# Softmax weights transposed by DMA in a window-attention and SoLU-MoE kernel

## The chip, the cores and the metric

The kernel runs on one core of a Trainium2 chip. Its time is the device time of one execution in microseconds, and the time before is the median of three runs. The profile comes from one further execution of the same program. TensorE is called PE there, its weight load PEld, VectorE DVE, ScalarE ACT, GpSimd POOL and SyncE SP; SP issues all DMAs of this kernel.

## The reference

A sliding-window attention (8 batches, 8 heads, 576 positions, head size 64, window 64) feeds a feed-forward block without residual (4608 tokens, 512 to 1024 to 512), all in float32:

```python
scores = scale * np.matmul(q, k.transpose(0, 1, 3, 2))
mask = (rel >= 0) & (rel < window)          # rel = pos[:, None] - pos[None, :], window = 64
scores = np.where(mask, scores, -1000000000.0)
scores = scores - np.max(scores, axis=-1, keepdims=True)
attn = np.exp(scores)
attn = attn / (np.sum(attn, axis=-1, keepdims=True) + 1e-09)
x = np.matmul(attn, v)                      # heads side by side: 4608 x 512
...
h = x @ w_in
e = np.exp(h - np.max(h, axis=-1, keepdims=True))
solu = h * e / (np.sum(e, axis=-1, keepdims=True) + 1e-09)
ln = (solu - mean) / np.sqrt(var + 1e-06) * g_ln
out = ln @ w_out
```

## The kernel before

The 4608 tokens are worked through in 36 tiles of 128. A query block of 64 sees 128 keys, so a tile's scores for one head are 128 x 128: two halves of 64 queries, each with its own shift of the keys and the values.

For each tile t the stages are these. **load** brings q (256 KB), k (384 KB) and two shifts of v (v0, v1, 256 KB each) by four DMAs. **scores** multiplies on TensorE into PSUM (pS). **softmax** takes row maxima on DVE (into sS), exponentials on ACT with row sums (sm), the reciprocal on DVE (rec), and scales sS head by head on POOL (L401). **transposes** turns the eight 128 x 128 heads on TensorE (t, L417), and ACT and DVE copy four each to SBUF (PT, L422). **values** multiplies PT with v into pX; ACT and DVE split the result into a rounded part xH and a rest xL. **moe_in** is two times 12 matmuls of 512 columns (high and low parts of x and of w_in) into pH. **moe_norm** is exp, product, squares and the layer norm, on DVE, ACT and POOL, and leaves e. **planes** takes e, 128 x 1024 float32, apart into two planes of 16-bit halves (pl; one half of the columns on DVE, one on POOL, L538). **turn** writes the planes to DRAM (yd, L545) and reads them back with a transposing DMA of 16-bit elements (yT, L548). **moe_transpose** splits yT into yH (ACT) and yL (DVE), **moe_out** is 24 matmuls into pO, ACT copies them to ot, and a DMA writes y.

The weights are 64-bit words in DRAM; eight blocks (raw, 1 MB each) are loaded and rebuilt as float32 by ACT and DVE at the start, and split into high and low parts a little later.

What sets the order is a planner, class `Plan`. Every stage is recorded with an engine, a cost in nanoseconds, the tiles it reads and writes, and a latency. Due times follow from the order on TensorE, and each engine's free slot goes to the ready work that is due first. Two lists were kept in the order of recording, TensorE's and SP's: `last` in `edges` holds both. `RINGS` gives the number of buffers of each tile. In the steady loop, iteration t records load(t+4), turn(t-1), the first half of moe_in(t), transposes(t+1), the second half, moe_norm(t) and planes(t), moe_transpose(t-2), values(t+1), scores(t+3), softmax(t+3) and moe_out(t-2).

Of the kernel before, what the change touches and what calls it, by code (L numbers as in the profile page):

```python
# [11 lines left out]
BF16 = mybir.dt.bfloat16  # L12
# [6 lines left out]
P = 128  # L19
# [25 lines left out]
}  # L47

# [1 line left out]
class Plan:  # L50
# [17 lines left out]
    def edges(self):  # L68

        before = [dict() for _ in self.ops]  # L70
        writer, readers, users, last = {}, {}, {}, {"PE": None, "SP": None}
        for i, (engine, _, _, reads, writes, _, loose) in enumerate(self.ops):
            for key in reads + writes:
                if key in writer:
                    before[i][writer[key]] = True
            for key in writes:
                for j in readers.pop(key, ()):
                    before[i][j] = True
                writer[key] = i
# [24 lines left out]
        return before  # L104
# [56 lines left out]
def tile_window_attention_solu_moe(  # L161
    ctx: ExitStack,
    tc: tile.TileContext,
    NBLK: int,
    qT: bass.AP,
    kT: bass.AP,
    v: bass.AP,
    w_in: bass.AP,
    w_out: bass.AP,
# [9 lines left out]

    nc = tc.nc  # L180

    NPAIR, _, NT = qT.shape
    DM = out.shape[1]
    w_in, w_out = w_in.bitcast(I32), w_out.bitcast(I32)
    DFF = w_in.shape[1] // 2
# [123 lines left out]

    def Q(t):
        return T("q", t, [P, NPAIR, P])

    def K(t):
        return T("k", t, [P, NPAIR, P + WIN])

    def V(t, half):
        return T(f"v{half}", t, [P, DM])

    def load(t, parts=range(4)):
        first = first_of(t)
        o = t * P

        lack = 0 if t else WIN
        if 0 in parts:
            plan.dma(P * P * 16, lambda: nc.sync.dma_start(
                Q(t), qT[:, :, o:o + P].rearrange("p d s -> d p s")), [], [("q", t)])
        if 1 in parts:
            plan.dma(P * P * 24, lambda: nc.sync.dma_start(  # L330
                K(t)[:, :, lack:], kT[:, :, o - WIN + lack:o + P].rearrange("p d s -> d p s")),
                [], [("k", t)])


        for half in range(2):
            i = o + (half - 1) * WIN
            if 2 + half not in parts:
                continue
            if first == half:
                for x in range(2):  # L340
                    plan.dma(P * P * 8, lambda x=x, half=half, i=i: nc.sync.dma_start(
                        V(t, half)[x * WIN:(x + 1) * WIN], v[i + WIN:i + P]),
                        [], [(f"v{half}", t, x)])
            else:
                plan.dma(P * P * 16, lambda half=half, i=i: nc.sync.dma_start(
                    V(t, half), v[i:i + P]), [], [(f"v{half}", t, x) for x in range(2)])
# [7 lines left out]
    def scores(t):  # L354
# [18 lines left out]
        plan.op("PE", 1000, emit, [("q", t), ("k", t)], [("pS", t)], loose=t < LOOSE)  # L373

    def softmax(t):
        def cols(tag, h):
# [23 lines left out]
        for h in range(H):  # L400
            plan.op(engine, cost, lambda h=h: v.tensor_scalar(  # L401
                SS(t)[:, h], SS(t)[:, h], rec()[:, h:h + 1], 0.0, ALU.mult, ALU.add),
                [("rec", t)], [("sS", t, h)])
# [30 lines left out]
    def values(t):  # L434
        def emit():
            for p in range(NPAIR):
# [46 lines left out]
    def moe_norm(t):  # L483
# [5 lines left out]
        def key(x):  # L489
# [42 lines left out]
    def planes(t):  # L532
        if not crosses(t):
            return
        for h in range(2):
            hs = slice(h * 512, (h + 1) * 512)
            engine, eng, cost = (("DVE", nc.vector, 1100), ("POOL", nc.gpsimd, 1300))[h]
            plan.op(engine, cost, lambda h=h, hs=hs, eng=eng: eng.tensor_copy(  # L538
                PL(t)[:, :, hs], E(t)[:, hs].bitcast(U16).rearrange("p (n k) -> p k n", k=2)),
                [("e", t, h)], [("pl", t, h)])  # L540

    def turn(t):
        if not crosses(t):
            return
        plan.dma(P * DFF * 4, lambda: nc.sync.dma_start(  # L545
            YD(t).rearrange("(p k) n -> p (k n)", k=2), PL(t).rearrange("p k n -> p (k n)")),
            [("pl", t, h) for h in range(2)], [("yd", t)])
        plan.op("SP", 4000, lambda: nc.sync.dma_start_transpose(  # L548
            YT(t).rearrange("p a b -> p (a b)").bitcast(U16).rearrange("p (a b) -> p a b", a=NF), YD(t)),
            [("yd", t)], [("yT", t)], 3000)  # L550

    def YH(t):
        return T("yH", t, [P, NF, P], F32 if t < PLAIN_OUT else F32R)
# [87 lines left out]
    for t in range(NTILE + BEHIND):  # L641
# [9 lines left out]
        if t < BEHIND:  # L651
            on(moe_in, t, 1)
            on(moe_norm, t)
            on(planes, t)
            on(transposes, t + 1)
            on(scores, t + AHEAD)
            on(softmax, t + AHEAD)
            on(values, t + 1)
        else:
            on(transposes, t + 1)  # L660
            on(moe_in, t, 1)
            on(moe_norm, t)
            on(planes, t)
# [47 lines left out]
```

## Time and profile before

| | |
|---|---|
| median of three runs | 571.24 us (570.96 to 571.53) |
| the profiled execution | 570.42 us, span 568.6 us |
| granted TensorE clock, mean | 0.985 |
| busy: PE, DVE, ACT, POOL | 537.1, 366.9, 322.1, 260.5 us |
| DMA: share of 16 engines by queue q1 | 57.1% |

A row of the groups reads: line, engine, operation, tile written <- tiles read, shapes, count | busy time in us, mean ns of one | idle time before it, and what ended that. A row of the chain: start, time, what. SPq rows are DMA issues: start, time of the issue on SP. A row of the windows: the stretch, its length, busy time of PE, PEld, DVE, ACT and POOL with counts, the granted clock, the DMA share and GB/s. Waits read: who waited <- for whom: total, times, longest.

### The profile page before, as it was taken

The page shows a single profiled execution, that of the slowest core. Times are in us where ns is not written, and L with a number is a line of the kernel's source. Part 1 is how long each engine was busy: PE and PEld are TensorE (multiplying, and loading weights), DVE is VectorE, ACT ScalarE, POOL GpSimd, SP SyncE. Part 2 cuts the span into 40 slices and gives each one's busy share as a digit, 9 for nine tenths or more (in the row PEclk, how much of TensorE's full clock was granted, in tenths as well). Part 3 has the DMA queues.
Part 4 walks back from the last instruction along what each step waited for, and adds up shares of the span by engine and source line. Part 5 has one row for each costly group of instructions (what it writes and reads, how often), then busy time and mean ns, then how long its engine had stood idle before and what let it go on. Part 6 is the DMA issues. An engine that isn't in the chain of part 4 may idle for free.

```text
span 568.6 us, 12131 instructions
## 1 busy us (share of the span) xinstructions
PE 537.1 (94%) x4312; PEld 420.1 (74%) x4312; DVE 366.9 (65%) x1198; ACT 322.1 (57%) x935; POOL 260.5 (46%) x439
## 2 busy tenths in 40 slices
PE   1587799999999999999999999999999999999997
PEld 1344368888888888888888888888888888888875
DVE  2968896666666666666666666666666666665540
ACT  3549785556555555555555555555555555554431
POOL 2036266554555545444455455555545555555310
PEclk9969799999999999999999999999999999999999
DMA  8967256556665565556766655556666655643310
GB/s 254 353 235 209 79 175 167 177 144 187 170 173 177 150 200 152 173 166 186 204 145 191 178 169 172 172 165 174 169 177 177 178 177 176 177 130 92 93 39 37
DMA packets 128956, 95.56 MB, mean 168 GB/s; under 512 B 72448, under 2 KB 109312, under 8 KB 128384
## 3 DMA queue, kind: packets, MB, share of 16 engines
q1 hardware_dynamic: 128896, 94.79, 57.1%
q8 instruction: 34, 0.56, 0.5%
q14 instruction: 26, 0.21, 0.1%
HBM read 50.73 MB, written 26.74 MB: 136 GB/s over the span
## 4 chain that ended last, share of the span: by engine, by line
PE 90%; DVE 3%; DMA 2%; POOL 1%; ACT 1%; SPq 1%; issue 0%; POOLq 0%
PE pO L606 36%; PE pH L478 33%; PE pS L369 6%; PE pX L441 6%; PE t L417 5%; PE pH L467 3%; DMA raw<-w_in 2%; POOL sS L401 1%; PE pO L596 1%; DVE w L286 1%; DVE sS L382 1%; DVE w L280 0%; DVE w L284 0%; DVE e L498 0%; ACT w L279 0%
## 5 line engine op out<-in xcount | busy, mean ns | idle before, releaser
L401 POOL TENSOR_SCALAR sS<-sS,rec 128x128 f32<-128x128 f32 x280 | 146.9, 542 | 52.2 <-DVE rec L398 29.1
L511 POOL TENSOR_TENSOR mst<-mst,neghalf 128x1 f32<-128x1 f32 x36 | 20.2, 561 | 234.2 <-DVE mst L509 234.2
L387 ACT ACTIVATE sS<-sS,nmx 128x128 f32<-128x128 f32 x288 | 112.3, 391 | 15.2 <-DVE nmx L382 15.0
L606 PE MATMUL pO<-w_outH,yH 128*128 128x512 f32 x280 | 114.7, 410 | 0.6 <-ACT yH L584 0.6
L606 PE MATMUL pO<-w,yH 128*128 128x512 f32 x280 | 110.9, 396 | 0.0
L606 PE MATMUL pO<-w_outH,yL 128*128 128x512 f32 x280 | 110.2, 394 | 0.0
L478 PE MATMUL pH<-w_inH,xH 128*128 128x512 f32 x264 | 107.9, 409 | 0.0
L478 PE MATMUL pH<-w,xH 128*128 128x512 f32 x264 | 103.9, 397 | 0.0
L478 PE MATMUL pH<-w_inH,xL 128*128 128x512 f32 x264 | 103.8, 393 | 0.0
L538 DVE COPY pl<-e 128x1024 uint16<-128x1024 uint16 x33 | 49.1, 1487 | 60.6 <-POOL e L515 60.6
L422 ACT COPY PT<-t 128x512 f32<-128x512 f32 x39 | 22.7, 587 | 93.9 <-PE t L417 93.9
L451 ACT CAST xH<-pX 128x512 fp32r<-128x512 f32 x33 | 19.3, 586 | 84.8 <-PE pX L441 84.8
L606 PEld LDWEIGHTS pO<-w_outH,yH 128*128 128x128 f32 x280 | 52.5, 187 | 17.8 <-issue 5.2
L606 PEld LDWEIGHTS pO<-w_outH,yL 128*128 128x128 f32 x280 | 52.6, 188 | 13.8 <-DVE yL L586 0.9
L515 POOL TENSOR_SCALAR e<-e,mst 128x512 f32<-128x512 f32 x72 | 58.1, 815 | 6.7 <-DVE mst L512 6.3
L606 PEld LDWEIGHTS pO<-w,yH 128*128 128x128 f32 x280 | 52.7, 188 | 10.8
L478 PEld LDWEIGHTS pH<-w_inH,xL 128*128 128x128 f32 x264 | 49.6, 188 | 12.5 <-issue 0.2
L493 DVE TENSOR_REDUCE mst<-pH 128x1 f32<-128x1024 f32 x36 | 44.0, 1222 | 22.9 <-PE pH L478 22.6
L478 PEld LDWEIGHTS pH<-w_inH,xH 128*128 128x128 f32 x264 | 49.6, 188 | 11.4 <-issue 0.2
L478 PEld LDWEIGHTS pH<-w,xH 128*128 128x128 f32 x264 | 49.7, 188 | 10.1
L369 PE MATMUL pS<-k,q 64*64 64x128 f32 x1152 | 42.4, 288 | 15.3 <-DVE sS L401 10.5
L387 ACT ACTIVATION_READ_ACCUMULATOR sS<-sS,nmx 128x1 f32 x288 | 54.1, 188 | 0.0
(66 smaller groups left out, 781.8 us busy)
## 6 DMA issues: line engine op xcount, KB each, us to landing
yd<-pl SPq DMA_DIRECT2D x33, 512.0 KB, 4.1
v<-vS SPq DMA_DIRECT2D x64, 256.0 KB, 3.4
k<-kT SPq DMA_DIRECT2D x35, 384.0 KB, 4.7
q<-qT SPq DMA_DIRECT2D x36, 256.0 KB, 4.0
y<-ot SPq DMA_DIRECT2D x36, 256.0 KB, 2.9
raw<-w_in SPq DMA_DIRECT2D x4, 1024.0 KB, 8.8
raw<-w_out SPq DMA_DIRECT2D x4, 1024.0 KB, 6.9
v<-vS SPq DMA_DIRECT2D x16, 128.0 KB, 3.2
```

The lines of the kernel that those rows point to most:

```text
L369: nc.tensor.matmul(PS(t)[half * WIN:(half + 1) * WIN, r, p], q[rs, p, half * WIN:(half + 1) * WIN], keys, start=True, stop=True)
L387: plan.op("ACT", 390, lambda h=h: nc.scalar.activation(SS(t)[:, h], SS(t)[:, h], AF.Exp, bias=cols("nmx", h), scale=-1.0, accum_out=cols(" ...
L401: plan.op(engine, cost, lambda h=h: v.tensor_scalar(SS(t)[:, h], SS(t)[:, h], rec()[:, h:h + 1], 0.0, ALU.mult, ALU.add), [("rec", t)], [( ...
L417: nc.tensor.transpose(pA()[:, i], SS(t)[:, 4 * x + i], ident)
L422: (nc.vector.tensor_copy if x and t >= EARLY else nc.scalar.copy)(PT(t)[:, 4 * x:4 * x + 4], pA()),
L441: nc.tensor.matmul(PX(t)[r * D:(r + 1) * D, p, ks], V(t, half)[:, h * D:(h + 1) * D], PT(t)[:, h, ks], start=True, stop=True)
L478: plan.op("PE", 233, lambda n=n, c=c, x=x, w=w: nc.tensor.matmul(PH(t)[:, hs], x(t)[:, c], WH(c, h) if w is WH else WL(c)[:, h], start=(n ...
L493: plan.op("DVE", 1150, lambda: nc.vector.tensor_reduce(nmax(), PH(t), axis=AX.X, op=ALU.max, negate=True), [("pH", t)], [key(0)])
L511: plan.op("POOL", 560, lambda: nc.gpsimd.tensor_tensor(kk(), kk(), neghalf, op=ALU.pow), [], [key(5)])
L515: plan.op("POOL", 770, lambda h=h, hs=hs: nc.gpsimd.tensor_scalar(E(t)[:, hs], E(t)[:, hs], nmean(), kk(), ALU.add, ALU.mult), [key(4), ke ...
L538: plan.op(engine, cost, lambda h=h, hs=hs, eng=eng: eng.tensor_copy(PL(t)[:, :, hs], E(t)[:, hs].bitcast(U16).rearrange("p (n k) -> p k n" ...
L606: plan.op("PE", 233, lambda f=f, i=i, x=x, k=k, y=y, w=w: nc.tensor.matmul(PO(), y(t)[:, f], w(i, x), start=(f == k == 0), stop=(f == NF - ...
```

## The change

From tile 4 on the softmax weights take the way that e takes already: POOL copies sS into two 16-bit planes (pp), a DMA writes them to DRAM (pd), and a transposing DMA reads them back as PT. The TensorE transposes and the copies out of PSUM are left out for these tiles. Both halves of the e planes go to DVE. q and k come as one array, laid out per tile on the host, in one DMA (qk, 640 KB); so do the two shifts of v (v, 512 KB). SP loses its fixed order in the planner. Some rings and planner costs change, and the squares of moe_norm go into the pl buffer instead of one of their own.

```diff
 BY_DMA = (1, 2)
+SOFT_BY_DMA = 4
 RINGS = {
-    "raw": 3, "w": 9, "q": 3, "k": 3, "v0": 3, "v1": 3, "sS": 3, "PT": 2, ...
-    "e": 3, "pl": 2, "yd": 3, "yT": 2, "sq": 1, ...
+    "raw": 3, "w": 9, "qk": 3, "v": 3, "sS": 2, "pp": 2, "pd": 3, "PT": 2, ...
+    "e": 2, "pl": 2, "yd": 3, "yT": 2, ...
...
-        writer, readers, users, last = {}, {}, {}, {"PE": None, "SP": None}
+        writer, readers, users, last = {}, {}, {}, {"PE": None}
...
+        if 0 in parts:
+            plan.dma(P * P * 40, lambda: nc.sync.dma_start(QK(t), qk[t]), [], [("qk", t)])
+        if 1 in parts:
+            plan.dma(P * P * 32, lambda: nc.sync.dma_start(T("v", t, [P, 2, DM]), v[t]), [], [("v", t)])
...
+    def soft_planes(t):
+        if t < SOFT_BY_DMA:
+            return
+        for x in range(2):
+            engine, copy, cost = ("POOL", nc.gpsimd.tensor_copy, 1050)
+            plan.op(engine, cost, lambda x=x, copy=copy: copy(
+                PP(t)[:, :, 4 * x:4 * x + 4].rearrange("p k h n -> p k (h n)"),
+                SS(t)[:, 4 * x:4 * x + 4].rearrange("p h n -> p (h n)").bitcast(U16).rearrange("p (n k) -> p k n", k=2)),
+                [("sS", t, 4 * x + i) for i in range(4)], [("pp", t, x)])
+
+    def soft_turn(t):
+        if t < SOFT_BY_DMA:
+            return
+        plan.dma(P * H * P * 4, lambda: nc.sync.dma_start(
+            PD(t).rearrange("(p k) n -> p (k n)", k=2), PP(t).rearrange("p k h n -> p (k h n)")),
+            [("pp", t, x) for x in range(2)], [("pd", t)])
+        plan.op("SP", 2600, lambda: nc.sync.dma_start_transpose(
+            PT(t).rearrange("p a b -> p (a b)").bitcast(U16).rearrange("p (a b) -> p a b", a=H), PD(t)),
+            [("pd", t)], [("PT", t, x) for x in range(2)], 2000)
...
     def transposes(t):
+        if t >= SOFT_BY_DMA:
+            return
...
-            T("sq", t, [P, DFF], BF16), E(t), AF.Square, bias=nmean(), scale=1.0, accum_out=ss()),
-            H2 + [key(4)], [key(3), ("sq", t)], lat=300)
+            PL(t)[:, 0].bitcast(BF16), E(t), AF.Square, bias=nmean(), scale=1.0, accum_out=ss()),
+            H2 + [key(4)], [key(3), ("pl", t, 0), ("pl", t, 1)], lat=300)
...
-            engine, eng, cost = (("DVE", nc.vector, 1100), ("POOL", nc.gpsimd, 1300))[h]
+            engine, eng, cost = ("DVE", nc.vector, 700)
...
-        plan.op("SP", 4000, lambda: nc.sync.dma_start_transpose(
+        plan.op("SP", 2600, lambda: nc.sync.dma_start_transpose(
...
-            [("yd", t)], [("yT", t)], 3000)
+            [("yd", t)], [("yT", t)], 2000)
...
             on(transposes, t + 1)
+            on(soft_turn, t + AHEAD - 1)
             on(moe_in, t, 1)
...
             on(softmax, t + AHEAD)
+            on(soft_planes, t + AHEAD)
```

The diff shows little of where the instructions land. Three places show it. The first is SP's queue in a steady iteration, of before; names carry the tile's number and then a buffer's:

```order
L345 DMA v0_16_2432<-vS 128x512
L345 DMA v1_16_2438<-vS 128x512
L545 DMA yd_11_2447<-pl_11_2363 128x2048
L548 DMA_TRANSPOSE yT_11_2465<-yd_11_2447 128x8x256
L614 DMA y<-ot_10_2499 128x512
L327 DMA q_17_2515<-qT 128x4x128
L330 DMA k_17_2522<-kT 128x4x192
```

And of the change:

```order
L327 DMA v_17_2471<-vS 128x1024
L405 DMA pd_15_2488<-pp_15_2457 128x2048
L325 DMA qk_19_2507<-qk 128x1280
L408 DMA_TRANSPOSE PT_15_2524<-pd_15_2488 128x8x256
L623 DMA y<-ot_11_2529 128x512
L554 DMA yd_13_2561<-pl_13_2509 128x2048
L557 DMA_TRANSPOSE yT_13_2593<-yd_13_2561 128x8x256
```

There are seven DMAs as before, but two transposing ones, each behind the write that feeds it; y moved ahead of yd, and one load stands between pd and PT.

The second place is DVE between the statistics of a tile and the row maximum of the next, of before:

```order
L507 SCALAR_TENSOR_TENSOR mst_12_2410<-mst_12_2410 128x1
L509 TENSOR_SCALAR mst_12_2410<-mst_12_2410 128x1
L395 TENSOR_SCALAR rec_15_2504<-sm_15_2454 128x8
L398 RECIPROCAL rec_15_2504<-rec_15_2504 128x8
L512 TENSOR_TENSOR mst_12_2410<-mst_12_2410 128x1
L538 COPY pl_12_2534<-e_12_2434 128x2x512
L422 COPY PT_14_2536<-t_57_2529 128x512
L574 TENSOR_TENSOR yL_11_2552<-yT_11_2465,yH_11_2541 128x512 x2
L493 TENSOR_REDUCE mst_13_2581<-pH_13_2495 128x1
```

And of the change:

```order
L516 SCALAR_TENSOR_TENSOR mst_13_2431<-mst_13_2431 128x1
L518 TENSOR_SCALAR mst_13_2431<-mst_13_2431 128x1
L583 TENSOR_TENSOR yL_12_2532<-yT_12_2433,yH_12_2519 128x512
L521 TENSOR_TENSOR mst_13_2431<-mst_13_2431 128x1
L583 TENSOR_TENSOR yL_12_2532<-yT_12_2433,yH_12_2519 128x512
L547 COPY pl_13_2509<-e_13_2459 128x2x512
L376 TENSOR_SCALAR rec_16_2553<-sm_16_2478 128x8
L547 COPY pl_13_2509<-e_13_2459 128x2x512
L379 RECIPROCAL rec_16_2553<-rec_16_2553 128x8
L502 TENSOR_REDUCE mst_14_2591<-pH_14_2522 128x1
```

The reciprocal of the softmax moved from ahead of the plane copies to behind them and behind yL; PT's copy is gone and a second plane copy has come.

The third is ACT in the change, from the exponential of moe_norm to the last exponential of the softmax:

```order
L504 ACTIVATE e_13_2459,mst_13_2431<-pH_13_2362,mst_13_2431 128x1024
L368 ACTIVATE sS_16_2467,sm_16_2478<-sS_16_2467,nmx_16_2468 128x128 x6
L513 ACTIVATE pl_13_2509,mst_13_2431<-e_13_2459,mst_13_2431 128x1024
L368 ACTIVATE sS_16_2467,sm_16_2478<-sS_16_2467,nmx_16_2468 128x128
L581 CAST yH_12_2519<-yT_12_2433 128x512
L622 COPY ot_11_2529<-pO_11_2463 128x512
L581 CAST yH_12_2519<-yT_12_2433 128x512
L368 ACTIVATE sS_16_2467,sm_16_2478<-sS_16_2467,nmx_16_2468 128x128
```

Before, all eight exponentials of a tile stood ahead of ot and yH; now the eighth stands behind both.

More of the change, by code (lines that the diff above doesn't have):

```diff
@@ L164, in tile_window_attention_solu_moe @@
     NBLK: int,
-    qT: bass.AP,
-    kT: bass.AP,
+    qk: bass.AP,
     v: bass.AP,
@@ L180, in tile_window_attention_solu_moe @@
     nc = tc.nc
-    NPAIR, _, NT = qT.shape
+    NTILE, NT, NPAIR = qk.shape[0], out.shape[0], qk.shape[2] // (2 * P + WIN)
     DM = out.shape[1]
@@ L308, in split, with QK, load @@
                 [("w", i), ("w", i, x), ("H", i, x)], [("w", NW + i, x)])
+    def QK(t):
+        return T("qk", t, [P, NPAIR * (2 * P + WIN)])
     def Q(t):
-        return T("q", t, [P, NPAIR, P])
+        return QK(t)[:, :NPAIR * P].rearrange("p (h s) -> p h s", h=NPAIR)
     def K(t):
-        return T("k", t, [P, NPAIR, P + WIN])
+        return QK(t)[:, NPAIR * P:].rearrange("p (h s) -> p h s", h=NPAIR)
     def V(t, half):
[L319 to L325, printed above, removed]
+        return T("v", t, [P, 2, DM])[:, half]
+    def load(t, parts=range(2)):
         if 0 in parts:
-            plan.dma(P * P * 16, lambda: nc.sync.dma_start(
-                Q(t), qT[:, :, o:o + P].rearrange("p d s -> d p s")), [], [("q", t)])
+            plan.dma(P * P * 40, lambda: nc.sync.dma_start(QK(t), qk[t]), [], [("qk", t)])
         if 1 in parts:
[L330 to L346, printed above, removed]
+            plan.dma(P * P * 32, lambda: nc.sync.dma_start(T("v", t, [P, 2, DM]), v[t]), [], [("v", t)])
     def SS(t):
@@ L371, in emit @@
                             q[rs, p, half * WIN:(half + 1) * WIN], keys, start=True, stop=True)
-        plan.op("PE", 1000, emit, [("q", t), ("k", t)], [("pS", t)], loose=t < LOOSE)
+        plan.op("PE", 1000, emit, [("qk", t)], [("pS", t)], loose=t < LOOSE)
     def softmax(t):
@@ L403, in softmax, with PP, PD @@
                 [("rec", t)], [("sS", t, h)])
+    def PP(t):
+        return T("pp", t, [P, 2, H, P], U16)
+    def PD(t):
+        return T("pd", t, [2 * P, H * P], U16, pool=dr)
+    def soft_planes(t):
[16 more added lines that the diff above has]
+            [("pd", t)], [("PT", t, x) for x in range(2)], 2000)
     def PT(t):
@@ L445, in values @@
         plan.op("PE", 1100, emit, [("PT", t, x) for x in range(2)]
-                + [(f"v{half}", t, x) for half in range(2) for x in range(2)], [("pX", t)],
+                + [("v", t)], [("pX", t)],
             loose=t < LOOSE)
@@ L618, in on @@
             f(t, *args)
-    load(0, range(2))
+    load(0, (0,))
     prep(0)
@@ L624, in tile_window_attention_solu_moe @@
     softmax(0)
-    load(0, range(2, 4))
+    load(0, (1,))
     prep(1)
@@ L660, in tile_window_attention_solu_moe @@
             on(transposes, t + 1)
+            on(soft_turn, t + AHEAD - 1)
             on(moe_in, t, 1)
@@ L667, in tile_window_attention_solu_moe @@
             on(softmax, t + AHEAD)
+            on(soft_planes, t + AHEAD)
             if t - BEHIND == PLAIN_OUT:
@@ L690 @@
     w_in, w_out, g = inputs["moe_w_in"], inputs["moe_w_out"], inputs["moe_g_ln"]
+    qT = q.transpose(1, 3, 0, 2).reshape(H // 2, 2 * D, B * S)
+    kT = k.transpose(1, 3, 0, 2).reshape(H // 2, 2 * D, B * S)
+    vS = v.transpose(0, 2, 1, 3).reshape(B * S, H * D)
+    tiles = _np.arange(B * S // P)[:, None] * P
+    keys = _np.maximum(tiles + _np.arange(-WIN, P), 0)
+    rows = tiles[:, :, None] + (_np.arange(2) * WIN - WIN) + _np.arange(P)[:, None]
+    fresh = (tiles[:, :, None] + _np.arange(2) * WIN) % S == 0
+    rows = _np.where(fresh & (_np.arange(P)[:, None] < WIN), rows + WIN, rows)
     ins = {
-        "qT": q.transpose(1, 3, 0, 2).reshape(H // 2, 2 * D, B * S),
-        "kT": k.transpose(1, 3, 0, 2).reshape(H // 2, 2 * D, B * S),
-        "vS": v.transpose(0, 2, 1, 3).reshape(B * S, H * D),
+        "qk": _np.concatenate([
+            qT.reshape(H // 2, 2 * D, -1, P).transpose(2, 1, 0, 3).reshape(-1, 2 * D, H // 2 * P),
+            kT[:, :, keys].transpose(2, 1, 0, 3).reshape(-1, 2 * D, H // 2 * (P + WIN))], 2),
+        "vS": vS[rows],
         "w_in": w_in.view(_np.int64),
```

1 line of the change is left out of this document (removed), and 4 rows, old and new, of the table RINGS.

## The prediction

> **What bounds the kernel now.** I read the page's shares and its chain first, then the chain in order of time for one steady tile, then the DMA queue of SP in the same stretch.
>
> ```profile
> PE 537.1 (94%) x4312; PEld 420.1 (74%) x4312; DVE 366.9 (65%) x1198; ACT 322.1 (57%) x935; POOL 260.5 (46%) x439
> PE 90%; DVE 3%; DMA 2%; POOL 1%; ACT 1%; SPq 1%; issue 0%; POOLq 0%
> ```
>
> TensorE is busy for 94% of the span and is 90% of the chain that ended last. The chain in order of time shows one tile without a gap:
>
> ```profile
> 137.90 2.82 PE pH L478 x12
> 140.72 0.87 PE t L417 x8
> 141.59 2.80 PE pH L478 x12
> 144.39 1.08 PE pX L441 x32
> 145.47 1.03 PE pS L369 x32
> 146.50 5.80 PE pO L606 x24
> 152.30 2.82 PE pH L478 x12
> ...
> 539.24 5.63 PE pH L478 x24
> ```
>
> One tile takes 152.30 - 137.90 = 14.40 us, of which the eight softmax transposes (t) take 0.87. The last row is a tile late in the program that has no transposes left between its two halves: 24 matmuls run straight through in 5.63 us, against 2.82 + 0.87 + 2.80 = 6.49. So taking the transposes out gives back all of their 0.86 to 0.87 us, if nothing else becomes the bound.
>
> What could become it is SP, which issues every DMA in order. One tile of its queue, from the timeline (start, time that the issue took):
>
> ```profile
> 318.27 0.82 SPq L345 DMA_DIRECT2D v<-vS  x2
> 319.19 0.37 SPq L545 DMA_DIRECT2D yd<-pl  x1
> 323.38 1.90 SPq L548 DMA_TRANSPOSE yT<-yd  x1
> 325.83 0.35 SPq L614 DMA_DIRECT2D y<-ot  x1
> 326.23 0.42 SPq L327 DMA_DIRECT2D q<-qT  x1
> 326.71 0.56 SPq L330 DMA_DIRECT2D k<-kT  x1
> ```
>
> The landings of yd and yT (microseconds from the start of the issue, least, middle, most; yd first), the time to landing of y, and the waits of SP:
>
> ```profile
> DMA to landing us min/median/max: 2.6/4.1/5.9
> DMA to landing us min/median/max: 4.1/4.3/5.7
> y<-ot SPq DMA_DIRECT2D x36, 256.0 KB, 2.9
> SPq L345 <- PE pX L441: 146.5, 28, 15.0
> SPq L548 <- DMA yd<-pl: 128.0, 33, 5.5
> ```
>
> SP cannot issue the transposing DMA before the write that feeds it has landed: 128.0 us of waiting in 33 tiles, 3.9 each. It has room for that today, for it stands another 146.5 us waiting for TensorE to free the value buffers.
>
> **The change part by part.**
>
> *Transposes off TensorE.* Tiles 4 to 35 lose 8 transposes each: 32 x 0.87 = 27.8 us. TensorE's tile becomes 14.40 - 0.87 = 13.53 us. Their two copies out of PSUM go too (one of ACT, one of DVE); neither engine bounds anything, so I count nothing.
>
> *A second round trip in the SP queue.* Each tile now writes the softmax planes to DRAM (pd, 512 KB, like yd) and reads them back through a transposing DMA (PT, the same shape as yT). The order on SP is v, pd, qk, PT, y, yd, yT, and both PT and yT stand there until the write before them has landed. I add up one turn from landing to landing, taking it that DMAs issued one behind the other land in their order. Then y cannot land before the PT ahead of it, and so on.
>
> The price of 512 KB that stands ahead in the queue comes from yd: it lands after 2.6 us at best, 4.1 in the middle, and what usually stands ahead of it is the two v loads, 512 KB together. That is 1.5 us. At the fullest rate that the DMA engines show it would be less (the columns after the clock are DMA share and GB/s):
>
> ```profile
> 321.60:322.08 0.48, 0.48 (x4) 0.38 (x3) 0.48 (x7) 0.21 (x2) 0.00 (x0) 1.00 1.04 427
> ```
>
> 512 KB at 427 GB/s are 1.23 us. I take 1.35 between the two, and 0.7 for 256 KB. One turn is then PT 4.3, y 0.7, yd 1.35, yT 4.3, v 1.35, pd 1.35: 13.35 us. This is made of middle values, and a chain without slack pays the mean. The mean wait of 3.88 us and the issue ahead of it (0.37) put yd's landing at 4.25 or a little more, some 0.2 over its middle; yT's most, 5.7, lies 1.4 over its middle. I add 0.2 for each of the two writes and 0.1 for each of the two transposes, 0.6 in all: **13.95 us**. That is 0.4 above TensorE's 13.53 and 0.45 below today's 14.40. So the queue, not TensorE, should set the pace.
>
> Bounds of this turn: 1.23 for each 512 KB, 0.6 for y and no jitter give 4.3 + 0.6 + 1.23 + 4.3 + 1.23 + 1.23 = 12.9, under TensorE's 13.53. With 1.5 for each 512 KB, 0.75 for y and the worst transposes they give 5.7 + 0.75 + 1.5 + 5.7 + 1.5 + 1.5 = 16.65.
>
> [...]
>
> *Fewer, larger loads.* q and k in one DMA, both shifts of v in another. SP issues 7 DMAs per tile before and after. In the packets only short ones go. qk (640 KB, 1.7 us by the price above) stands between pd and PT in the queue. It should be hidden: the transposing DMA issued at 323.38 moves nothing for 1.1 us (DMA share 0.00 until 324.48, rows below), and pd's landing is told some time after its last packet, while qk already moves. If not hidden, it costs up to 1.7 - 1.1 = 0.6 per turn. The engines' load itself fits:
>
> ```profile
> 324.00:324.48 0.48, 0.48 (x4) 0.38 (x3) 0.36 (x2) 0.48 (x3) 0.00 (x1) 1.00 0.00 0
> 324.48:324.96 0.48, 0.48 (x4) 0.38 (x3) 0.17 (x1) 0.24 (x2) 0.48 (x1) 1.00 0.33 78
> 324.40:326.90 2.50, 2.50 (x12) 1.99 (x11) 0.43 (x3) 0.91 (x3) 2.09 (x4) 1.00 0.97 215
> 350.00:400.00 50.00, 50.00 (x392) 40.30 (x391) 31.07 (x115) 28.63 (x89) 25.06 (x41) 1.00 0.62 174
> ```
>
> 0.62 x 14.40 = 8.9 us per tile today, and 1.35 for pd and 2.5 x 0.97 = 2.4 for PT make 12.7, less what the short packets cost. It is under 13.53, though not by much.
>
> *Planes and softmax.* POOL gives its half of the e planes to DVE and gets two copies of the softmax planes (1.04 us each, by its own copy below).
>
> ```profile
> 312.77 1.04 POOL L538 COPY pl<-e 128x1024 uint16<-128x1024 uint16 x1
> 312.87 1.50 DVE L538 COPY pl<-e 128x1024 uint16<-128x1024 uint16 x1 [2.06 <-POOL e L515]
> L401 POOL TENSOR_SCALAR sS<-sS,rec 128x128 f32<-128x128 f32 x280 | 146.9, 542 | 52.2 <-DVE rec L398 29.1
> L398 DVE RECIPROCAL rec<-rec 128x8 f32<-128x8 f32 x36 | 7.3, 202 | 1.0
> L401 POOL TENSOR_SCALAR sS<-sS,rec x280: 364/374/1392, 29.5 to 518.4; 128x128 f32<-128x128 f32 x140
> L572 ACT CAST yH<-yT 128x512 fp32r<-128x512 f32 x66 | 37.9, 621 | 4.8 <-DMA yT<-yd 3.6 <-issue 1.1
> L574 DVE TENSOR_TENSOR yL<-yT,yH 128x512 fp32r<-128x512 f32 x66 | 44.7, 714 | 8.4 <-ACT yH L572 8.2
> L613 ACT COPY ot<-pO 128x512 f32<-128x512 f32 x36 | 21.1, 585 | 26.9 <-PE pO L606 26.9
> ```
>
> DVE's copy ends 0.56 us after POOL's (314.37 against 313.81), so I read it as 0.94 of standing behind POOL and 0.56 of work; two on DVE are then 1.1 us where POOL is idle, and at most 3.0, the upper end for rival C. [...]
>
> This makes a second ring of waits. ACT and DVE now take yH and yL of the tile before in the middle of the softmax, and the last exponential stands behind ot. From the end of one moe_out: ot 0.59, yH 0.62, yL 0.71, two plane copies 1.12, reciprocal 0.20, eight scalings 8 x 0.374, two soft planes 2.08, pd 4.1, PT 4.3, and then pX, pS and pO 7.91 bring the moe_out two tiles later: 24.6 us over two tiles, 12.3 each. With the scalings at their mean of 0.542, plane copies 1.5 and soft planes as slow as that, it is 28.7, or 14.4 each. I take a value near 13.2, since half of the scalings take at most 374 ns: below the queue's 13.95.
>
> *Start.* SP's order is free now, so the four w_in blocks are loaded earlier, with the first queries behind the first block. The chain there holds:
>
> ```profile
> 4.19 10.84 DMA raw<-w_in
> 50.59 5.10 POOL sS L401 x8
> ```
>
> Weights earlier by some 2 us, scores later by some 3 (1 MB at the start); these rows give no sign, so 0, with 3 us either way.
>
> **Sum.** Some 28 tiles run with the full queue: 28 x (14.40 - 13.95) = 12.6 us. The last four have no loads and go at TensorE's pace: 4 x 0.87 = 3.5. The profiled execution took 570.42 us (span 568.6), so 570.4 - 16.1 = 554.3. The median of the runs, 571.24, is 0.8 above it; I forecast **554** for the time, the start being uncertain by more than that.
>
> **The rivals.**
>
> A, TensorE keeps the pace: the queue's turn stays under 13.53 (its low bound is 12.9), and all 27.8 us come: 570.4 - 27.8 + 0.8 = 543. For it: the middle values alone make 13.35. Against it: no slack to swallow any jitter.
>
> B, my forecast, 13.8 to 14.1 per tile: 550 to 559.
>
> C, the softmax ring decides at 14.2: 28 x 0.2 + 3.5 = 9.1, so 562. For it: scalings of up to 1392 ns. Against it: it needs nearly all upper values at once.
>
> D, slower: the queue's turn passes 14.40 because qk stands ahead of PT (0.6) and transposes land late beside other traffic, 0.4 more on average; 13.95 + 1.0 = 14.95 gives 28 x 0.55 - 3.5 = 11.9 lost, 583. The point from which it decides is a turn 0.57 over my sum. For it: landings of 5.7 exist. Against it: middle and least lie 0.2 apart.
>
> **How the numbers follow.** B 0.48, A 0.22, C 0.10, D 0.15, and 0.05 for landing on no change, within 0.2% (about what a measurement of this kernel can tell). Faster is A, B and C less a little of B's edge: 0.79; same 0.05; slower 0.16. The range goes from just under A, 542, to 570, beyond C and to where D begins.
>
> **What would show it.** In the profile after: pH's 24 matmuls in one piece of 5.63 in the chain; tiles of 13.9 us in the chain; SP with hardly any wait left for TensorE (146.5 now), and waiting for pd and yd nearly 4 us twice per tile; TensorE standing before pX for PT, some 0.4 us per tile. If that stand is missing and the tile is 13.5, A was right; if SP still waits for POOL's pp, C; if tiles exceed 14.4 with PT landing over 5 us, D. A pd or PT that lands without regard to what was issued ahead of it would break the sum itself.

## The result, and the profile after

The changed kernel takes 589.88 us (median; 589.24 to 591.6), the kernel before 571.18 us beside it: a ratio of 1.033, with a 95% interval of 1.031 to 1.036. It is 18.7 us slower. The forecast was 554 us in a range of 542 to 570; it was wrong, also in the sign.

From the page of the changed kernel: busy times, the DMA queue, and the chain that ended last (by engine, then by line).

```profile
PE 513.4 (87%) x4056; PEld 397.1 (68%) x4056; DVE 341.1 (58%) x1199; ACT 303.0 (52%) x903; POOL 279.3 (48%) x470
...
q1 hardware_dynamic: 161920, 128.47, 73.8%
...
DMA 40%; PE 25%; SPq 14%; POOL 7%; DVE 6%; issue 3%; ACT 3%; POOLq 0%; ACTq 0%
DMA pd<-pp 22%; PE pO L615 13%; DMA yd<-pl 13%; SPq L557 7%; PE pH L487 5%; SPq L408 4%; DMA PT<-pd 4%; POOL e L524 3%; POOL sS L382 3%; PE pH L476 2%; PE pX L450 2%; PE pS L350 2%; SPq L327 2%; SPq L623 1%; DVE yL L583 1%
```

TensorE's busy time fell by 23.7 us (537.1 before), so the transposes are gone as meant. But TensorE is now 25% of the chain, where it was 90%, and the two writes to DRAM with SP's issues make up nearly half of it. The chain in order of time shows one turn of SP's queue without a gap (start, time, what):

```profile
329.80 1.91 SPq L557
331.71 0.05 issue
331.81 0.53 SPq L327
332.34 0.04 issue
332.43 6.08 DMA pd<-pp
338.53 1.91 SPq L408
340.44 0.05 issue
340.53 0.53 SPq L623
341.06 0.05 issue
341.15 3.57 DMA yd<-pl
344.74 1.94 SPq L557
```

L557 issues yT, L327 v, L408 PT, L623 y. From one yT to the next are 344.74 - 329.80 = 14.94 us, and no engine that computes is in it: SP issues yT and v, pd lands 6.08 us after its issue, only then PT can be issued, then y and yd, and yd lands after 3.57. SP's waits of the same kernel (who waited <- for whom: total, times, longest):

```profile
SPq L408 <- DMA pd<-pp: 152.0, 32, 6.2
SPq L557 <- DMA yd<-pl: 101.1, 32, 4.6
SPq L327 <- PE pX L450: 24.1, 3, 16.9
```

And the longest of TensorE's:

```profile
PE pX L450 <- DMA PT<-pd: 32.2, 21, 2.3
```

Where SP once waited 146.5 us for TensorE, TensorE now waits for SP's queue. The landings of the DMAs (KB each, median us from issue):

```profile
qk<-qk SPq DMA_DIRECT2D x36, 640.0 KB, 7.4
v<-vS SPq DMA_DIRECT2D x36, 512.0 KB, 5.6
yd<-pl SPq DMA_DIRECT2D x33, 512.0 KB, 3.6
pd<-pp SPq DMA_DIRECT2D x32, 512.0 KB, 6.1
y<-ot SPq DMA_DIRECT2D x36, 256.0 KB, 2.9
```

**Where the 18.9 us of span went** (587.5 against 568.6), worked out from the starts of the tiles' scores on TensorE: the scores of tile 5 start 7.7 us earlier (64.5 against 72.2); from there to the scores of tile 8 it takes 53.9 instead of 44.4, 9.5 more; the next 25 tiles take 15.12 each instead of 14.41, 17.8 more; the next two 1.0 more, and the end 1.8 less.

**The turn by its steps.** The medians of the landings, each counted from the landing before it in the queue: PT 4.3, y 0.6, yd 1.3, yT 4.2, v 3.3, pd 1.3, together 15.0. The prediction had 4.3, 0.7, 1.35, 4.3, 1.35, 1.35. One term differs: v, by 2 us. (It ranges from 1.7 to 3.9 in the single tiles.)

### The profile page after: what moved, and what is told of

Its sections match the earlier page's. It is cut to its first block, busy times and chain, and to the rows that moved or that the text cites. A ratio compares the mean times of both kernels' runs of the same rounds, so it can differ in the third digit from the quotient of the medians.

```text
span 587.5 us, 11562 instructions
## 1 busy us (share of the span) xinstructions
PE 513.4 (87%) x4056; PEld 397.1 (68%) x4056; DVE 341.1 (58%) x1199; ACT 303.0 (52%) x903; POOL 279.3 (48%) x470
## 4 chain that ended last, share of the span: by engine, by line
DMA 40%; PE 25%; SPq 14%; POOL 7%; DVE 6%; issue 3%; ACT 3%; POOLq 0%; ACTq 0%
DMA pd<-pp 22%; PE pO L615 13%; DMA yd<-pl 13%; SPq L557 7%; PE pH L487 5%; SPq L408 4%; DMA PT<-pd 4%; POOL e L524 3%; POOL sS L382 3%; PE pH L476 2%; PE pX L450 2%; PE pS L350 2%; SPq L327 2%; SPq L623 1%; DVE yL L583 1%
## 5 line engine op out<-in xcount | busy, mean ns | idle before, releaser
L382 POOL TENSOR_SCALAR sS<-sS,rec 128x128 f32<-128x128 f32 x280 | 105.0, 400 | 75.8 <-DVE rec L379 26.4
L615 PE MATMUL pO<-w_outH,yH 128*128 128x512 f32 x280 | 116.4, 416 | 8.6 <-ACT yH L581 8.0
L615 PE MATMUL pO<-w,yH 128*128 128x512 f32 x280 | 112.8, 403 | 0.0
L524 POOL TENSOR_SCALAR e<-e,mst 128x512 f32<-128x512 f32 x72 | 87.0, 1215 | 51.8 <-DVE mst L521 51.4
L487 PE MATMUL pH<-w_inH,xH 128*128 128x512 f32 x264 | 105.4, 399 | 0.0
L583 DVE TENSOR_TENSOR yL<-yT,yH 128x512 fp32r<-128x512 f32 x66 | 47.7, 726 | 51.8 <-ACT yH L581 51.8
L450 PE MATMUL pX<-PT,v 128*64 128x64 f32 x1152 | 42.5, 227 | 39.5 <-DMA PT<-pd 32.2
L450 PEld LDWEIGHTS pX<-PT,v 128*64 128x64 f32 x1152 | 38.1, 140 | 53.2 <-issue 47.5
L547 DVE COPY pl<-e 128x1024 uint16<-128x1024 uint16 x66 | 46.2, 702 | 34.4 <-POOL e L524 34.4
L397 POOL COPY pp<-sS 128x1024 uint16<-128x1024 uint16 x64 | 64.9, 1048 | 0.0
L615 PEld LDWEIGHTS pO<-w_outH,yL 128*128 128x128 f32 x280 | 53.7, 192 | 15.1 <-DVE yL L583 1.0
```

The lines of the kernel that those rows point to most:

```text
L382: plan.op(engine, cost, lambda h=h: v.tensor_scalar(SS(t)[:, h], SS(t)[:, h], rec()[:, h:h + 1], 0.0, ALU.mult, ALU.add), [("rec", t)], [( ...
L397: plan.op(engine, cost, lambda x=x, copy=copy: copy(PP(t)[:, :, 4 * x:4 * x + 4].rearrange("p k h n -> p k (h n)"), SS(t)[:, 4 * x:4 * x + ...
L450: nc.tensor.matmul(PX(t)[r * D:(r + 1) * D, p, ks], V(t, half)[:, h * D:(h + 1) * D], PT(t)[:, h, ks], start=True, stop=True)
L487: plan.op("PE", 233, lambda n=n, c=c, x=x, w=w: nc.tensor.matmul(PH(t)[:, hs], x(t)[:, c], WH(c, h) if w is WH else WL(c)[:, h], start=(n ...
L524: plan.op("POOL", 770, lambda h=h, hs=hs: nc.gpsimd.tensor_scalar(E(t)[:, hs], E(t)[:, hs], nmean(), kk(), ALU.add, ALU.mult), [key(4), ke ...
L583: plan.op("DVE", 620, lambda hs=hs: nc.vector.tensor_sub(YL(t)[:, hs], YT(t)[:, hs], YH(t)[:, hs].bitcast(F32)), [("yT", t), ("yH", t, h)] ...
```

## The experiments

Three theories stood at first. **T**: the turn of SP's queue sets the pace, and it is too long because the load v stands between yT and pd. **R1**: a ring of waits through DVE, ACT and POOL sets it (the reciprocal stands behind yL on DVE, which waits for yT), and the queue only shows it. **R2**: v, as one load of 512 KB, takes 3.36 us by itself, wherever it stands. The kernel before took 570.3 to 570.8 us beside the experiments.

### Without the softmax by DMA

```diff
-SOFT_BY_DMA = 4
+SOFT_BY_DMA = 36
```

> The change without its main part: no tile's softmax weights go by DMA (SOFT_BY_DMA = 36), all other parts stay. Theory T (the turn of the SP queue with two transposing DMAs sets 15.05 us per tile in the change, and 2 us of it are a load that starts late behind a transposing DMA): with one transposing DMA per tile the queue has slack, TensorE sets 14.40 us per tile, 570 us, 566 to 573. Rival R1 (the softmax path through POOL, DVE and ACT sets the pace, with the reciprocal now behind the plane copies) expects part of the loss to stay: 575 to 585. Rival R2 (a 512 KB load of v in one DMA takes 3.36 us by itself) expects 570 too.

563.76 us, ratio 0.987 (0.985 to 0.989). The other parts of the change gain by themselves, all of it at the start: tile 5 starts at 64.5 as in the change, and tiles take 14.41 as before. So the loss of the change comes in with the softmax by DMA. The gain begins with the first weights. From the chain of this kernel:

```profile
0.73 4.87 DMA raw<-w_in
```

The first weight block of w_in is there at 5.6 us and the fourth at 15.6; before, they landed at 10.8 and 23.5 (the row 4.19 10.84 in the prediction is the second block). The 7.9 us by which the fourth is earlier are near the 7.7 us gained.

### v behind pd

SP's finished order is changed at one place, here as in the runs below:

```diff
+        sp = [i for i in out if self.ops[i][0] == "SP"]
+        for n, i in enumerate(sp):
+            if tag(i) == "v" and "pd" in map(tag, sp[n + 1:n + 4]):
+                j = next(j for j in sp[n + 1:n + 4] if tag(j) == "pd")
+                out.remove(i)
+                out.insert(out.index(j) + 1, i)
```

> The change with one DMA moved: v is issued behind pd, not ahead of it, so that a store and not a load stands right behind yT. T: the turn of the queue becomes PT 4.3 and some 1.2 for v and qk that now stand ahead of it, y 0.6, yd 1.3, yT 4.2, pd 1.3, together 12.9; TensorE's 13.53 sets the pace: 545 to 553 us, pd lands some 1.3 after yT. R1: nothing changes, 587 to 590. R2: v costs its 3.36 in the new place and stands ahead of PT: 585 to 592.

562.78 us, ratio 0.986 (0.983 to 0.990); tiles of 14.17. One DMA in another place takes 27 us off the change, which neither R1 (587 to 590) nor R2 (585 to 592) allows. It is not the 37 or more that T forecast either: with v right behind it pd lands 1.8 behind yT in the middle, where T had 1.3, and PT, with two loads ahead of it, 5.7 after its issue, where T had 5.5 and the change has 4.3. What makes the rest of the 14.17, over the 12.9 of T, is open.

### y behind yT, ahead of v

```diff
+            if tag(i) == "y" and "yT" in map(tag, sp[n + 1:n + 4]):
+                j = next(j for j in sp[n + 1:n + 4] if tag(j) == "yT")
```

> The change with y moved from behind PT to right behind yT, ahead of v. T: y moves while the load behind it could not have moved anyway, so its 0.6 us leave the turn: 14.45 us per tile, 570 to 574 us. R1 and R2: y is paid in another place or does not matter, 587 to 590.

586.37 us, ratio 1.027 (1.024 to 1.031); a miss, for T expected 570 to 574. A store ahead of v does not use up the time in which v is late: y lands 0.7 behind yT and v still 2.7 behind y.

### Half of v

```diff
-        return T("v", t, [P, 2, DM])[:, half]
+        return T("v", t, [P, 2, DM])[:, half if t < 9 else 0]
...
-            plan.dma(P * P * 32, lambda: nc.sync.dma_start(T("v", t, [P, 2, DM]), v[t]), [], [("v", t)])
+            plan.dma(P * P * 32, lambda: nc.sync.dma_start(
+                T("v", t, [P, 2, DM])[:, :2 if t < 9 else 1], v[t][:, :2 if t < 9 else 1]), [], [("v", t)])
```

> The change with the second shift of v not loaded from tile 9 on (256 KB in place of 512; values uses the first shift for both halves, so that part is left out). T: the 2 us before the load moves stay, 0.65 us of data go: 14.4 us per tile, 570 to 576 us. R2: 3.36 is a rate, half of it goes: 13.5 us per tile, 546 to 556. R1: 587 to 590.

558.68 us, ratio 0.979 (0.976 to 0.981); tiles of 14.06. 256 KB less give back 1.06 us per tile, half as much again as the 0.7 that the prediction's price gives for these bytes: half of v lands 1.5 behind yT. The time lies between the 546 to 556 of R2 and the 570 to 576 of T; neither had it.

### v behind yd

```diff
+            if tag(i) == "v" and "pd" in map(tag, sp[n + 1:n + 2]) and "yd" in map(tag, sp[n + 1:n + 7]):
+                j = next(j for j in sp[n + 1:n + 7] if tag(j) == "yd")
```

> The change with v issued behind yd, where the queue waits for yd's landing and the next transposing DMA starts up. Theory T2 (the turn of the SP queue sets the pace as long as it is over TensorE's 13.53; a load costs nothing where it moves while a write's landing is awaited and a transposing DMA starts, and costs most right behind a transposing DMA): the turn becomes PT 4.3, y 0.6, yd 1.3, yT 4.4, pd 1.3 to 1.8, together 12.0 to 12.5, so TensorE sets 13.53: 27 tiles x (14.17 - 13.53) less than the run with v behind pd, 543 to 550 us. Rival R1 (the softmax path with its waits takes over at once): 556 to 563.

552.04 us, ratio 0.968 (0.966 to 0.970). Here v is issued while SP waits for yd anyway; nothing else differs from the change. SP's timeline of one turn (start, time of the issue):

```profile
327.31 1.94 SPq L567 DMA_TRANSPOSE yT<-yd  x1
329.35 0.53 SPq L415 DMA_DIRECT2D pd<-pp  x1
329.93 0.42 SPq L335 DMA_DIRECT2D qk<-qk  x1
333.44 2.96 SPq L418 DMA_TRANSPOSE PT<-pd  x1
336.49 0.53 SPq L633 DMA_DIRECT2D y<-ot  x1
337.11 0.38 SPq L564 DMA_DIRECT2D yd<-pl  x1
337.54 0.44 SPq L337 DMA_DIRECT2D v<-vS  x1
340.63 2.51 SPq L567 DMA_TRANSPOSE yT<-yd  x1
```

And from this kernel's landings:

```profile
pd<-pp SPq DMA_DIRECT2D x32, 512.0 KB, 3.6
```

pd lands after 3.6 us instead of 6.1, and yT follows yT after 13.32 instead of 14.94. The place of this one load costs 589.88 - 552.04 = 37.8 us, twice the whole loss. T's main point is borne out, that the place of v sets the pace, though 552.04 lies above its 543 to 550; the tiles of 13.83 (TensorE's own would be 13.5) leave something to a second cause, below.

### Why v is late: split, pieces, a store ahead

```diff
-            plan.dma(P * P * 32, lambda: nc.sync.dma_start(T("v", t, [P, 2, DM]), v[t]), [], [("v", t)])
+            plan.dma(P * P * 32, lambda: [nc.sync.dma_start(V(t, half), v[t][:, half]) for half in range(2)],
+                     [], [("v", t)])
```

> The change with v loaded by two DMAs of 256 KB (2 KB per partition each), both where the one of 512 KB stands, right behind yT. The place is the same, the bytes are the same. If the late start behind yT comes with the 4 KB rows or the larger DMA (theory M, the merged load): both halves land within 2.2 us of yT and the turn falls to some 13.9 us, 555 to 562 us. If it belongs to the place (theory T): the turn stays at 15 us, 585 to 592.

582.76 us, ratio 1.022 (1.019 to 1.024): two DMAs as before the change help a little, and do not take the loss away. Of the landings M was nearly right: the halves land 1.6 and 2.4 behind yT in the middle, so v as a whole comes about 1 us sooner than in one DMA. But the tiles still take 14.81, for yT, PT and yd land 0.1 to 0.2 later on average. Why they do stays open.

```diff
+            plan.dma(P * P * 32, lambda: nc.sync.dma_start(
+                T("v", t, [P, 2, DM]), v[t].rearrange("a p n -> p a n")), [], [("v", t)])
...
-        "vS": vS[rows],
+        "vS": vS[rows].transpose(0, 2, 1, 3),
```

> The change with v laid out so that its one DMA of 512 KB reads pieces of 2 KB. If the piece's size makes the late start (M, by size of a piece): 555 to 562 us. If it is the DMA's size (M, by size of a DMA) or the place (T): 585 to 592.

589.61 us, ratio 1.034 (1.030 to 1.037): the layout of v in DRAM is not it either.

```diff
-        plan.op("SP", 2600, lambda: nc.sync.dma_start_transpose(
-            YT(t).rearrange("p a b -> p (a b)").bitcast(U16).rearrange("p (a b) -> p a b", a=NF), YD(t)),
-            [("yd", t)], [("yT", t)], 2000)
+        plan.op("SP", 2600, lambda: nc.sync.dma_start(
+            YD(t).rearrange("(p k) n -> p (k n)", k=2), PL(t).rearrange("p k n -> p (k n)")),
+            [("pl", t, h) for h in range(2)], [("yd", t), ("yT", t)], 2000)
```

> The change with the transposing DMA yT replaced by a second store of the same 512 KB to the same place, which waits for yd's landing as yT did; v stands behind it as before, and yH and yL are made from resident weights instead of yT (so the second product computes something else). It measures the disputed term alone: how long after the DMA ahead of it v lands. If the late start belongs to a transposing DMA just ahead (T): v lands 1.2 to 1.7 us behind the store. If any first load after stores starts that late (rival L): 2.5 to 3.4 us. The time itself falls in both cases, since the store lands sooner than yT: under T some 545, under L some 565.

552.29 us in one run; v lands 1.9 behind the store in the middle of its cases (1.2 to 3.6). This lies between both theories: later than its bytes, but not as late as behind yT. The run changes a second thing, though: pd is issued 1.9 us behind v in the middle of its cases, and 0.6 in the change. So it doesn't separate what stands ahead of v from what follows it.

### The DMAs by themselves

What was still open is whether v is late by its place behind a transposing DMA or by what follows it. Behind the last store of the changed kernel, groups of the same DMAs ran with nothing else on the core, three times each:

```diff
+PROBE = ("v", "yd v", "yd yT v", "yd yT wait v", "yd yT v0", "yd yT pd", "yd yT v pd", "yd yT pd v")
...
+        for name in PROBE * 3:
...
+            for x in name.split():
+                if x == "yd":
+                    nc.sync.dma_start(yd.rearrange("(p k) n -> p (k n)", k=2), pl.rearrange("p k n -> p (k n)"))
...
+                elif x == "v":
+                    nc.sync.dma_start(vt, v[n % 36])
+                elif x == "v0":
+                    nc.sync.dma_start(vt[:, 0], v[n % 36][:, 0])
```

> The changed kernel, with a tail behind its last store in which the DMAs of a tile run by themselves, each group waiting until everything of the group before has landed, three times each: the load v alone; v behind the write yd; v behind the transposing yT; v issued only when yT has landed; half of v behind yT; the write pd behind yT; v and then pd behind yT; pd and then v behind yT. Its time is only that of the change plus the tail and says nothing. Q (it belongs to the queue by itself: a load that stands right behind a transposing DMA starts late): v lands 2.8 to 3.4 behind yT also here, where nothing else runs; pd there lands 1.2 to 1.6 behind yT; v behind yd 1.5 to 2.0 behind it. N (it belongs to the neighbours: v shares the engines with the pd issued right behind it, or with the other traffic of the tile): v lands 1.2 to 1.6 behind yT by itself, and 2.8 to 3.4 only where pd follows it. Under both, pd and then v behind yT lands as a whole 1 us earlier than v and then pd only if Q holds.

| behind yT | landing behind the landing of yT |
|---|---|
| v | 1.9, 2.0, 2.2 |
| half of v | 1.1, 1.3, 0.9 |
| pd | 1.2, 1.1, 1.2 |
| v, then pd | v 3.4, 2.9, 3.3; pd 4.6, 4.1, 4.5 |
| pd, then v | pd 1.6, 1.9, 1.7; v 3.1, 3.8, 3.2 |

Behind yd, v lands 2.0, 1.7 and 1.8 later. With nothing beside it v lands 3.3 to 3.6 after its issue, and 3.1 to 3.2 when it is issued only after yT has landed. v without pd lands 1.9 to 2.2 behind yT: later than N's 1.2 to 1.6, but far from Q's 2.8 to 3.4. It takes 2.9 to 3.4, as in the kernel, only when pd is issued right behind it. That is N's mark: behind yT, the write that follows costs the load 0.7 to 1.5 us, 1.3 in the middle. It is not the same with every DMA that follows. In the run without the softmax by DMA the load qk (640 KB) is issued 0.6 us behind v, and v lands 2.1 behind yT in the middle (1.2 to 3.5), as it does by itself. And half of v lands 1.5 behind yT in the kernel, with pd behind it, against 0.9 to 1.3 here.

The expectation that the other order lands 1 us earlier only under Q was wrong; it lands earlier here (3.1 to 3.8 against 4.1 to 4.6, in the middle 3.2 against 4.5), so the two orders of one pair are not alike. One pair of v and then pd, the first of the three, with its landings (KB, us from issue):

```profile
v<-vS SPq DMA_DIRECT2D x1, 512.0 KB, 5.8
pd<-pp SPq DMA_DIRECT2D x1, 512.0 KB, 6.4
yT<-yd SPq DMA_TRANSPOSE x1, 4.4
```

Its two issues in the timeline of SP:

```profile
642.20 0.57 SPq L712 DMA_DIRECT2D v<-vS  x1
642.83 0.42 SPq L716 DMA_DIRECT2D pd<-pp  x1
```

And the windows behind them (stretch, length, busy time of PE, PEld, DVE, ACT and POOL, granted clock, DMA share, GB/s):

```profile
644.50:645.00 0.50, 0.00 (x0) 0.00 (x0) 0.00 (x0) 0.00 (x0) 0.00 (x0) 0.50 0.59 139
645.00:645.50 0.50, 0.00 (x0) 0.00 (x0) 0.00 (x0) 0.00 (x0) 0.00 (x0) 0.50 0.35 139
645.50:646.00 0.50, 0.00 (x0) 0.00 (x0) 0.00 (x0) 0.00 (x0) 0.00 (x0) 0.50 0.92 369
646.00:646.50 0.50, 0.00 (x0) 0.00 (x0) 0.00 (x0) 0.00 (x0) 0.00 (x0) 0.50 0.92 377
646.50:647.00 0.50, 0.00 (x0) 0.00 (x0) 0.00 (x0) 0.00 (x0) 0.00 (x0) 0.50 1.00 410
647.00:647.50 0.50, 0.00 (x0) 0.00 (x0) 0.00 (x0) 0.00 (x0) 0.00 (x0) 0.50 0.82 336
647.50:648.00 0.50, 0.00 (x0) 0.00 (x0) 0.00 (x0) 0.00 (x0) 0.00 (x0) 0.50 0.37 148
```

v is issued at 642.20 and lands 5.8 later, at 648.0; yT landed at 644.6. From 644.5 to 648.0 the engines move 0.5 x (139 + 139 + 369 + 377 + 410 + 336 + 148) = 959 thousand bytes in these rows. v has 524 thousand, so at least 435 thousand are pd's: most of pd's bytes move before v has landed. How v's own bytes lie between them, the rows don't tell. And in the first microsecond only 139 GB/s move, where later 410 do. By itself behind yT v also starts slowly, with 188 GB/s in the first half microsecond, but moves 426 in the next.

Why the same pair is cheaper in the other order, no run here shows; nor why a load behind v does not make it late, nor whether pd right behind v would do so behind a store in yT's place.

With the middle of this pair, 4.5, and the landings of the change for the rest, the turn nearly closes: PT 4.3, y 0.6, yd 1.3, yT 4.2 and the pair are 14.9, against tiles of 15.12.

### The entry and the second cause

With v behind yd, as above, and:

```diff
-SOFT_BY_DMA = 4
+SOFT_BY_DMA = 8
```

> The run with v behind yd, but the softmax weights go by DMA from tile 8 on, not 4. Asked: what are the 10 us that tiles 6 to 8 lose at the entry. If they belong to the start, where DVE and ACT still split the weights (rival S): they vanish, four tiles at 14.40 cost 3.5, so 544 to 548 us. If they belong to the entry into the longer path itself, wherever it stands, with the reciprocal waiting behind yL for yT (theory W): they move to tiles 10 to 12, 553 to 558 us.

545.96 us, ratio 0.957 (0.953 to 0.961). From the scores of tile 5 to those of tile 8 it takes 45.5 instead of 54.4: the loss at the entry goes away when the DMA way starts four tiles later, and at the later entry only one tile is long, with 16.0. That the collision with the end of the weights' work on DVE and ACT makes it is argued, not shown.

The next has v behind yd too, `SOFT_BY_DMA = 4`, and on ACT the last exponentials of a softmax right ahead of yH, on DVE the reciprocal and the last factor of moe_norm right ahead of yL (`ahead` moves an operation as far as what it needs allows):

```diff
+        for i in [i for i in out if self.ops[i][0] == "ACT" and ("sm", 0) <= self.ops[i][4][-1][:2] and self.ops[i][4][-1][0] == "sm"
+                  and self.ops[i][4][-1][1] >= 5]:
+            ahead(i, "yH", 0)
+        for i in [i for i in out if self.ops[i][0] == "DVE" and tag(i) in ("rec", "mst") and self.ops[i][4][0][1] >= 5]:
+            ahead(i, "yL", 0)
```

> The run with v behind yd, and with the last exponential put ahead of yH on ACT and the reciprocal and the last factor of moe_norm ahead of yL on DVE, so that the softmax and POOL do not wait for yT of the tile before. Theory W (that wait makes the entry loss and the unsteady tiles at 13.83): the entry loses at most 3 us in place of 10, tiles come to 13.55, 536 to 543 us. Rival (both come from the SP queue alone): 549 to 554.

550.6 us, ratio 0.965 (0.964 to 0.967), above the 536 to 543 expected: the loss at the entry stays (56.4 us from tile 5 to tile 8). But the steady tiles were as W had them, and the chain in order of time has nothing but TensorE in it:

```profile
329.45 5.63 PE pH L512 x24
335.07 1.08 PE pX L475 x32
336.15 1.03 PE pS L375 x32
337.19 5.80 PE pO L640 x24
342.99 2.12 PE pH L512 x9
```

342.99 - 329.45 = 13.54 us a tile, where v behind yd alone had 13.83. The two profiles make the difference look large: they are of the shortest execution here (548.23) and of the longest there (554.91), and the medians are only 1.4 us apart (550.6 and 552.04). So R1's ring is there, but second, and worth at most 0.3 us a tile once the queue is out of the way. The exponential, the reciprocal and the factor were moved together; which of them counts is not shown.

Both together are this kernel with `SOFT_BY_DMA = 8`:

> This is e10_rec_early (v issued behind yd, the last exponential ahead of yH, the reciprocal and the last scaling ahead of yL), with the softmax weights by DMA only from tile 8 on. Two effects were measured one at a time: the reciprocal's place took the steady tile from 13.83 to 13.54 (theory W, for the steady tiles), and the later start took the loss of some 10 us out of tiles 5 to 8 (theory S: the start of the transposing collides with the end of the weights' preparation). If both hold and add: tiles 5 to 8 take 45 to 46, tiles from 9 on 13.5 to 13.6, first tile at 64 to 65, 541 us (538 to 544). If they don't add (the loss at the entry moves to tile 8 with the new order, or the steady tile goes back to 13.8): 544 to 548.

546.29 us, ratio 0.957 (0.952 to 0.961), in the median no better than without the early reciprocal: so far as it can be told, the two gains do not add. Two of the four executions took 543.2 and 544.6, two 548.0 and 548.1; in the profiled one, of 548.1, it took 47.3 from tile 5 to tile 8, and one tile behind them took 18.4. This version and the one with v behind yd from tile 8 are the fastest measured, 24 to 25 us under the kernel before and some 44 under the change.

### SP's order fixed again

```diff
-        writer, readers, users, last = {}, {}, {}, {"PE": None}
+        writer, readers, users, last = {}, {}, {}, {"PE": None, "SP": None}
```

> The changed kernel with the issue order of SyncE's queue fixed again as the program is written (yT, pd, PT, y, qk, v, yd in a tile); all else as in the change. The theory of the queue's turn (T) with what was measured so far: yT 4.2, pd behind it 1.5, PT 4.3, y 0.6, qk as the first load behind a transposing DMA 2.8, v behind a load 1.3, yd 1.3, in sum 16.0 a tile, 0.9 more than in the change: 605 to 615 us. The rival (the order of SyncE's queue doesn't matter, since the same seven DMAs are in it): 587 to 592, tile 15.0 to 15.2. It tells one more thing: whether the 7.7 us gained at the start belong to the free order (the first softmax tile of the piece-wise kind then starts at 72 us again) or to the merged loads (it stays at 64.5).

655.61 us, ratio 1.150 (1.148 to 1.153): far slower than either theory had. SP's timeline of a tile:

```profile
334.30 2.01 SPq L557 DMA_TRANSPOSE yT<-yd  x1
336.72 0.35 SPq L405 DMA_DIRECT2D pd<-pp  x1
340.37 2.14 SPq L408 DMA_TRANSPOSE PT<-pd  x1
342.62 0.52 SPq L623 DMA_DIRECT2D y<-ot  x1
343.19 0.42 SPq L325 DMA_DIRECT2D qk<-qk  x1
346.98 0.33 SPq L327 DMA_DIRECT2D v<-vS  x1
347.40 0.38 SPq L554 DMA_DIRECT2D yd<-pl  x1
```

And of SP's waits the one for TensorE:

```profile
SPq L327 <- PE pX L450: 112.0, 31, 13.4
```

Here v's buffer comes free only with pX, which waits for PT, so v is issued 3.8 us behind qk, and yd stands behind it. The landings, here at their means in the steady tiles, add up to yT 4.3, pd 1.2, PT 4.4, y 0.7, qk 2.4, v 3.1, yd 1.4, 17.5; the tiles took 17.49. The turn's sum holds; the expected 16.0 had no wait for TensorE in it. The free order is thus a help to this change and not its fault. Of the 7.7 us at the start, 4.6 remain in the fixed order (tile 5 at 67.6); the fourth w_in block lands at 18.9 there, 4.6 us earlier than before. So the free order is worth 3.1 of them; what makes the other 4.6, the merged loads or another part, was not taken apart.

## Why the prediction was wrong

- **TensorE's tile, 13.53 without the transposes: right.** pH runs in one piece of 5.63 us where nothing holds it, and the tile is 13.54 in the version with an early reciprocal.
- **SP's queue becomes the bound: right**, with the signs that were named: the waits for TensorE nearly gone, two waits for pd and yd in each tile, TensorE standing before pX for PT.
- **The turn of 13.95: this step failed**, at one term, "v 1.35". It measured 3.3, and the tiles 15.12. The term was priced by v's own bytes, from a case where loads stood ahead of a write. Alone behind yT it takes 1.9 to 2.2; the pd issued right behind it adds 0.7 to 1.5. The assumption that "DMAs issued one behind the other land in their order" held (none of the 247 of the change lands ahead of the one issued before it); that each then costs only its own bytes did not. pd's and yd's terms were right within 0.1, yT and PT too. With v at 3.3 the sum without jitter is 15.3, and the prediction's own 28 tiles then give 28 x (15.3 - 14.4) - 3.5 = 21.7 us lost: this one term turns the sign.
- **qk hidden: right.** It lies between pd and PT, and PT still lands 4.3 behind its issue. In the turn shown above 344 GB/s move on average from 334.50 to 338.50, 1376 thousand bytes; v and pd have 1049, so at least 327 thousand of qk's have moved by pd's landing. With v there as well it is hidden no more (5.7).
- **The softmax ring, 13.2 in 12.3 to 14.4: right that it lies below the queue.** The chain of the change goes through POOL, DVE and ACT for 16% of the span, the start included. Once the queue is mended, it costs at most 0.3 us a tile. One of its terms was small: a plane copy on DVE took 0.69 us in the middle, not 0.56. The 0.56 was the author's estimate from the end of POOL's copy; beside that copy DVE's took 1.50 in the middle in the kernel before.
- **The start at 0: wrong by 7.7 us**, a gain, beyond the 3 us that were allowed either way. The weights were given 2 us; the fourth block of w_in came 7.9 us earlier.
- **Not foreseen**: 9.5 us lost from tile 5 to tile 8. It and the gain at the start nearly cancel, by luck.
- **The rivals.** The outcome is on D's side, and its 583 and its turn of 14.95 were near 590 and 15.1. That was luck, for its reason was another: neither was qk the price, nor do transposes land late (4.2 and 4.3 in the middle, where its sign was a PT over 5). The tiles lie beyond the point from which it decides, 0.57 over the sum. The mechanism, a load that lands later for the write behind it, was not among the rivals.

## What to carry to other kernels

When a queue holds two write-and-read-back trips per tile and stands before each read-back until the write has landed, as SP did here for 152.0 and 101.1 us, add up one turn from landing to landing and ask of each DMA in it whether it could stand where the queue waits anyway; moving one 512 KB load there was worth 37.8 us. Do not price a load by its own bytes when it stands between a transposing DMA and a write: in this kernel's probe the pair of load and write took 4.1 to 4.6 us there, and 3.1 to 3.8 in the other order. And look at what an engine's order hangs on a late transfer: moving an exponential, a reciprocal and a factor ahead of it was worth up to 0.3 us a tile, though only once the queue was mended.

## What was unexpected of the hardware

Of two DMAs in one queue, the first can land later because of the second: a load of 512 KB lands 1.9 to 2.2 us behind a transposing DMA by itself, and 2.9 to 3.4 with a 512 KB write issued 0.6 us behind it. With a load of 640 KB behind it instead it lands 2.1 behind in the middle. The reverse order of the two is cheaper here: both have landed 3.1 to 3.8 us behind the transposing DMA, against 4.1 to 4.6. A load that stands first behind yT or behind a write takes 0.4 to 0.9 us more than the 1.3 that 512 KB take as a write behind it; a write behind yT shows no such excess (1.1 to 1.2 for 512 KB).
